# Threshold attention and a gelu feed-forward on one core: the row thresholds of ten score tiles move from adding DMAs to VectorE, under a new set of planner ranks

## The chip, the cores and the metric

The kernel runs on one core of one Trainium2 chip. The time is device microseconds from launch to the last store, taken as the median of several executions. A profiled execution gives the span from the first to the last instruction and what each engine did in it: PE (TensorE; its weight loads are PEld), DVE (VectorE), ACT (ScalarE), POOL (GpSimd) and SP (SyncE). SP and POOL mostly issue DMAs here, each from its own queue.

## The reference

Two stages in fp32. Attention has 8 batches of 8 heads, 576 positions and a head dimension of 64; a score below its row's maximum less tau is dropped before the softmax. Its output, seen as 4608 tokens of 512 values, goes through a feed-forward of width 2048.

```python
scores = scale * np.matmul(q, k.transpose(0, 1, 3, 2))
thresh = np.max(scores, axis=-1, keepdims=True) - tau
scores = np.where(scores >= thresh, scores, -1000000000.0)
scores = scores - np.max(scores, axis=-1, keepdims=True)
attn = np.exp(scores)
attn = attn / (np.sum(attn, axis=-1, keepdims=True) + 1e-09)
...
h = x @ w_in
g = h * (1.0 / (1.0 + np.exp(-1.702 * h)))
return (g @ w_out).astype(np.float32)
```

## The kernel before

**Tiling.** Heads go in pairs n = 0 to 31, four pairs to a batch (`NPAIR`). A pair's transposed scores lie in five tiles t = 0 to 4 in SBUF: four of 128x1152 and a last one of 128x576, half as large ("full" and "half" tiles below).

**One pair's steps.** `load_qk` and `load_v` (SP) bring q, k and v in. For pairs 0 to 3 PE turns q and k (`turn_in`, L566/L569), ACT evacuates q's turn (`turned`, L581) and DVE k's (L579). `scores_run` (PE, L591) makes nine pieces of scores, and `keep` (ACT, L608) copies each out of PSUM. `in_groups` (DVE, L614) takes maxima within each tile, `over_tiles` (L623) over the tiles; `cross_max` (ACT, L633) and `over_halves` (DVE, L640) combine across partitions. The result is each query's threshold. It then reaches all partitions in one of two ways. For most pairs DVE spreads it (`spread_max`, L652). For the pairs in `BY_DMA` (1, 3, 4, 5, 6) DVE turns it to a negated row (`turn_rows`, L647/L648), one DMA stores the row to DRAM (`row_out`, L664) and another reads it back to every partition (`row_in`, L673).

Then comes the step that the change touches: the threshold is taken from every score tile. `sub` (L688) does it on DVE, in place, with the spread threshold as the second operand (an add for the `BY_DMA` pairs, whose row is negated). `add_row` (L679) does it without DVE: POOL issues two DMAs that read the row from DRAM and accumulate it onto the tile in SBUF. The dictionary `ADDED` names the tiles that go that way: tiles 3 and 4 of pairs 1, 3, 4, 5 and 6.

After it `mask` (ACT, L695) sends negative differences far down, `exps` (ACT, L699) takes the exponential, and PE multiplies with v and with ones (`values` and `sums_by_pe`, L710). For pairs 0 to 3 `one_row` (DVE, L741) makes the reciprocal sums and `place_x` (DVE, L814) writes the four blocks of the scaled output where the feed-forward reads its x. PE's feed-forward can begin with a batch's tokens when all four of its pairs are placed.

**Weights.** They come in pieces, packed as pairs of 16-bit halves, and are put together by ACT and DVE: `load_w` (SP), `cv_power` (ACT, L521), `cv_power2` (ACT, L525), `cv_whole` (DVE, L539) and `cv_end` (DVE, L546), in this chain for every piece; `cv_whole` needs the load alone, `cv_end` both others.

**Feed-forward.** Tokens go in 18 blocks of 256. The first two are one group: PE L877/L888 (first product, 16 columns j of the hidden layer, two of which fit PSUM at a time), ACT tanh (L844), DVE `gelu_0` (L894), PE L857 (second product). Later blocks use products of sums and differences of half matrices (L956, L1098, L1397, and L1249 and L1358 for the last four), which need further sums by DVE (L1144, L1263 on ACT, L1266 and others) and prepared weights that POOL moves (`t_minus` L998, `t_plus` L1002, `w_plus` L927, `w_flow` L1075).

**What sets the order.** The schedule is manual. Each step is a task with an engine, an estimated cost, a rank, what it comes after and which buffers it takes and gives. `run_in_order` plays the tasks through once while the program is built: whenever an engine is free in this model, the ready task of lowest rank whose buffers are free is emitted on it. The engines then run what was emitted, each in its own order. A rank is a pair's number plus a bias by the step's name, from one of three dictionaries, `EARLY` for pairs 0 to 3, `SECOND` for pairs 4 to 7 and `LATER` for the rest; `CV` holds the biases of the weight steps, `W_RANK` the ranks of the pieces by groups, `L_RANK` those of the loads of q, k and v of the first eight pairs. So one list of numbers decides where every step stands among the others on its engine:

```python
biases = EARLY if a[0] < NPAIR else SECOND if a[0] < 2 * NPAIR else LATER
rank += CV[f.__name__] if f.__name__ in CV else biases.get(f.__name__, 0.0)
```

and the tile's way is chosen where the tasks of a pair are listed:

```python
if t in mine:
    last_add = task("POOL", 1.3, r, add_row, n, t, after=[last_add] + copies)
    a = transfer("DMW", 2.0 if tail else 4.0, last_add, 1, lag=2.0, ...)
else:
    a = task("DVE", 0.67 if tail else 1.27, r, sub, n, t, after=[y for y, _ in subs], ...)
```

(`mine` is `ADDED.get(n, ())`.) The buffer of the row in DRAM (`row`, one) is given back by the last add of a pair in `ADDED`, and by the transfer of `row_in` for any other; the buffer of the spread threshold is given back by the pair's last `sub`.

Of the kernel before, what the change touches and what calls it, by code (L numbers as in the profile page):

```python
# [32 lines left out]
def kernel(  # L33
# [97 lines left out]
    for x in ("raw0", "raw1", "qkT0", "qkT1", "mb"):  # L131
# [3 lines left out]


    EARLY = {
        "add_row": -35.07,
        "cross_max": 51.78,
        "exps": -47.2,  # L140
        "in_groups": 31.96,
        "keep": 48.24,
        "load_qk": -22.72,
        "load_v": -16.59,
        "mask": 58.66,
        "one_row": 92.6,
        "over_halves": -5.3,
        "over_tiles": 3.55,
        "place_x": -34.81,
        "row_in": -3.02,  # L150
        "row_out": 179.21,
        "scores_run": -83.61,
        "spread_max": -0.55,
        "spread_sums": 83.81,
        "sub": 80.72,
        "sums_by_pe": 70.37,
        "turn_in": 65.21,
        "turn_rows": -10.62,
        "turned": 53.23,
        "values": -17.63,  # L160
    }
    SECOND = {
        "add_row": 6.96,
        "cross_max": 30.38,
        "cross_sums": 55.52,
        "exps": 48.43,
        "in_groups": 180.71,
        "keep": -68.97,
        "load_qk": -48.26,
        "load_v": -36.2,  # L170
        "mask": 36.98,
        "over_halves": -6.02,
        "over_tiles": 2.67,
        "place_x": 82.5,
        "prep": 45.44,
        "row_in": -45.04,
        "row_out": 99.69,
        "scores_run": 89.89,
        "spread_max": 152.36,
        "sub": 70.1,  # L180
        "sums_in": -66.2,
        "sums_out": 19.25,
        "turn_rows": -3.9,
        "turn_sums": 85.81,
        "values": 27.28,
    }
    LATER = {
        "add2": 28.57,
        "add3": -10.19,
        "copy2": 7.59,  # L190
        "copy3": 128.37,
        "cross_max": 33.26,
        "cross_sums": -30.68,
        "exps": 4.78,
        "in_groups": 26.34,
        "keep": -16.52,
        "load_qk": 26.97,
        "load_v": 0.95,
        "mask": -12.52,
        "over_halves": 1.14,  # L200
        "over_tiles": -27.28,
        "place_x": -12.29,
        "prep": 220.24,
        "s_level1": 112.72,
        "s_level2": 77.75,
        "scores_run": -3.6,
        "silu2": 34.02,
        "spread_max": 18.84,
        "sub": -15.73,
        "sums_in": 49.27,  # L210
        "sums_out": 57.21,
        "turn_sums": 100.25,
        "values": -2.28,
    }
    CV = {
        "cv_end": 87.96,
        "cv_power": 26.67,
        "cv_power2": -7.18,
        "cv_whole": 151.72,
        "load_w": 4.18,  # L220
    }

    LAG = {"PE": 0.26, "DVE": 0.18, "ACT": 0.22, "POOL": 0.18, "SP": 0.1}
# [7 lines left out]
    def task(engine, cost, rank, f, *a, after=(), take=(), give=(), lag=None):  # L231
        if lag is None:
            lag = LAG[engine]
        if rank != FIRST and rank < LAST and f not in (first_act, tau_terms, run_up, stay_warm):
            biases = EARLY if a[0] < NPAIR else SECOND if a[0] < 2 * NPAIR else LATER
            rank += CV[f.__name__] if f.__name__ in CV else biases.get(f.__name__, 0.0)
        tasks.append((engine, cost, rank, f, a, [x for x in after if x is not None],
                      take, give, lag))
        return len(tasks) - 1
# [9 lines left out]
    def transfer(by, time, a, kind=0, give=(), lag=1.7):  # L249
        return task(by, time, FIRST, moved, kind, after=[a], give=give, lag=lag)  # L250
# [182 lines left out]
    def own(n, *pools):  # L433
        return tuple(x + "_apart" for x in pools) if n in APART else pools
# [1049 lines left out]

    SUMS_IN_A = 2
    SUMS_BY_PE = (0, 1, 2, 3)
    ADDED = {n: (3, 4) for n in (1, *range(3, 7))}
    BY_DMA = (1, *range(3, SINGLE))
    SUMS_BY_DMA = range(4, NP)
    LEAD = 6  # L1490
# [4 lines left out]
    FFU = 1.727  # L1495
    T_RANK = FIRST

    W_RANK = (-2.54, 76.74, 38.5, 60.86, -18.31, 3.32)
    W_TIME = 1.8
    WARM = 22  # L1500
    ROUND_BY_ACT = range(0)
# [2 lines left out]
    for i in range(len(pieces)):  # L1504
        y = 0 if i < NDC else 2 if i < n_in else 4
        n = NDC if i < NDC else n_in - NDC if i < n_in else n_in
        first = (0, 0, NDC, 0, n_in)[y]
        rank = W_RANK[y] + (W_RANK[y + 1] - W_RANK[y]) * (i - first) / n
        if not wide:
# [732 lines left out]
            next_blk += 1  # L2242

    crossed = {"max": [], "sums": []}
    L_RANK = (-36.67, -8.83, 19.0, 14.55, -8.83, 6.12, -80.2, -13.57, 33.56, 28.6, 36.68, 5.08, 89.16, -23.31, -89.41, -12.49, 50.76, 2.25, -31.08, -35.43, 70.85, 84.46, 108.91, -12.25)

    def load_rank(n, which):
        return L_RANK[3 * n + which] if 3 * n < len(L_RANK) else 0.0

# [15 lines left out]
    for n in range(NP):  # L2265
# [106 lines left out]
        if n in BY_DMA:  # L2372
            a = task("DVE", 0.22, r, turn_rows, n, after=[a])
            a = transfer(rq[2], 0.3 + 0.4 * by_sp, task(rq[0], 0.65 * rq[1], r, row_out, n, after=[a]), lag=1.7 - 0.4 * by_sp + flow)
            spread[n] = task(rq[0], 1.1 * rq[1], r, row_in, n, after=[a], take=own(n, "mb"))
            m = transfer(rq[2], 1.1, spread[n], 0 if by_sp else 1, give=() if n in ADDED else ("row",), lag=rq[3] + flow)
        else:
            m = task("DVE", 0.78, r, spread_max, n, after=[a], take=own(n, "mb"))
        spread.setdefault(n, m)
        ws, subs, last_add = [], [(m, None)], spread[n]  # L2380
        mine = ADDED.get(n, ())
        for t in range(NKT + 1):
# [108 lines left out]
```

## Time and profile before

| | |
|---|---|
| median of 3 runs | 1229.73 us (1229.53 to 1229.79) |
| profiled execution, its own time | 1230.11 us |
| its span | 1228.3 us, TensorE clock 0.999 |
| PE busy | 1212.3 us (99%) |
| PEld busy | 980.9 us (80%) |
| DVE busy | 1059.2 us (86%) |
| ACT busy | 817.5 us (67%) |
| POOL busy | 71.2 us (6%) |
| `sub`, L688 | 150 instructions, 180.2 us |
| `mask`, L695 | 160 instructions, 164.2 us |
| `add_row`, L679 | 20 DMA issues, 18.9 us busy, from 35.9 to 167.8 us; 4.5 to 11.9 us from issue to landing, median 7.8 |
| `row_in`, L673 | 10 DMA issues, 5.3 us busy |

"Busy" is the time in which an engine executes an instruction; "idle before" is the time it stood still ahead of one. DVE's and ACT's records overlap by some 0.08 us when one instruction follows another directly, so the distance of starts says what an instruction costs its engine, not its length. Times within the span are counted from its start. In lists by stretch, the columns after a stretch's length are the busy times of PE, PEld, DVE, ACT and POOL, each with its number of instructions in brackets, then the granted TensorE clock, the mean busy share of the 16 DMA engines and the GB/s they moved; a share above 1 in such a list means that more transfers were under way than there were engines.

### The profile page before, as it was taken

What the parts mean: (1) busy time and instruction counts of PE and PEld (TensorE: products, weight loads), DVE (VectorE), ACT (ScalarE), POOL (GpSimd) and SP (SyncE); (2) the same over time, 40 slices, a digit from 0 to 9 for tenths busy, and PEclk for the clock granted to TensorE, in tenths of its full rate; (3) what the DMA queues carried; (4) which work ended last, traced back from release to release, by engine and by line L of the source; (5) the groups of instructions that cost most, each with busy time, mean ns of one, the idle gap of its engine ahead of it and who ended that gap; (6) DMA issues with size and microseconds to landing.
All of it is one profiled execution on the core that took longest, in us unless ns stands there. A gap on an engine that the chain in (4) does not pass through costs nothing.

```text
span 1228.3 us, 26047 instructions
## 1 busy us (share of the span) xinstructions
PE 1212.3 (99%) x10592; PEld 980.9 (80%) x10592; DVE 1059.2 (86%) x1650; ACT 817.5 (67%) x1203; POOL 71.2 (6%) x115
## 2 busy tenths in 40 slices
PE   9988999999999999999999999999999999999998
PEld 6746764497978888888777777777887797999998
DVE  6998984779898998899699987998789889999797
ACT  7999995786766766685776467756875677340330
POOL 0111213110000000000000010000100000000000
PEclk9999999999999999999999999999999999999999
DMA  7956858793323133224423252224322342344443
GB/s 220 250 109 175 189 122 159 135 210 73 110 49 110 39 92 85 75 74 130 102 66 101 73 129 74 65 64 120 99 49 66 112 113 61 118 131 137 146 126 106
DMA packets 201512, 137.12 MB, mean 112 GB/s; under 512 B 146800, under 2 KB 163184, under 8 KB 201264
## 3 DMA queue, kind: packets, MB, share of 16 engines
q1 hardware_dynamic: 188992, 110.21, 33.4%
q0 software_dynamic: 11712, 24.95, 9.9%
q8 instruction: 83, 1.36, 0.5%
q10 hardware_dynamic: 688, 0.30, 0.1%
q14 instruction: 37, 0.30, 0.1%
HBM read 103.28 MB, written 23.75 MB: 103 GB/s over the span
## 4 chain that ended last, share of the span: by engine, by line
PE 85%; ACT 7%; DVE 5%; DMA 1%; issue 1%; ACTq 0%; DVEq 0%
PE ops L1397 24%; PE pv L710 10%; PE ps L591 10%; PE hps L956 7%; PE hps L1098 7%; PE ps L956 5%; PE ps L1098 5%; PE ops L857 5%; PE ops L1358 3%; PE hps L1249 3%; PE ps L1358 2%; PE ps L1249 2%; DVE arena L1266 2%; PE hps L888 2%; ACT arena L699 2%; ACT arena L695 2%
## 5 line engine op out<-in xcount | busy, mean ns | idle before, releaser
L614 DVE TRANSPOSE_TENSOR_REDUCE part<-arena 128x36 f32<-128x1152 f32 x300 | 364.0, 1240 | 54.2 <-ACT arena L608 43.3
L608 ACT COPY arena<-ps 128x576 f32<-128x576 f32 x288 | 170.4, 644 | 107.8 <-PE ps L591 107.5
L695 ACT ACTIVATE arena<-arena 128x1152 f32<-128x1152 f32 (+1 forms) x160 | 164.2, 1059 | 49.3 <-DVE arena L688 46.0
L699 ACT ACTIVATE arena<-arena,shift,scl 128x1152 f32<-128x1152 f32 (+1 forms) x160 | 193.9, 1245 | 1.2
L688 DVE TENSOR_TENSOR arena<-arena 128x1152 f32<-128x1152 f32 (+1 forms) x150 | 180.2, 1243 | 0.7
L591 PE MATMUL ps<-arena 64*64 64x288 f32 x2304 | 171.1, 408 | 4.0 <-ACT arena L608 3.5
L1397 PE MATMUL ops<-w_out,arena 128*128 128x256 f32 x768 | 174.5, 381 | 0.0
L1397 PEld LDWEIGHTS ops<-w_out,arena 128*128 128x128 f32 x768 | 144.2, 190 | 25.3 <-issue 5.7
L710 PE MATMUL pv<-arena 64*64 64x288 f32 x2176 | 159.7, 405 | 0.0
L591 PEld LDWEIGHTS ps<-arena 64*64 64x64 f32 x2304 | 82.6, 133 | 65.6 <-ACT arena L608 23.8
L710 PEld LDWEIGHTS pv<-arena 64*64 64x64 f32 x2176 | 82.3, 133 | 52.2 <-issue 8.8
L1397 PE MATMUL ops<-arena 128*128 128x256 f32 x528 | 118.1, 379 | 0.0
L1397 PEld LDWEIGHTS ops<-arena 128*128 128x128 f32 x528 | 100.2, 190 | 14.0 <-issue 0.4
L1263 ACT COPY arena<-hps 128x512 f32<-128x512 f32 x44 | 25.7, 583 | 58.5 <-PE hps L1249 44.3
L633 ACT ACTIVATE other<-red,minus_gap 32x18 f32<-32x18 f32 x118 | 36.2, 307 | 34.3 <-DVE red L623 32.7
L857 PE MATMUL ops<-w_out,arena 128*128 128x512 f32 x128 | 55.9, 595 | 0.0
L1075 POOL DMA_DIRECT2D arena<-wrow x36 | 19.4, 540 | 595.9 <-DVE arena L688 298.6
L888 PE MATMUL hps<-xT,w_in 128*128 128x256 f32 x232 | 51.7, 382 | 2.0 <-DVE arena L894 1.9
L888 PEld LDWEIGHTS hps<-xT,w_in 128*128 128x128 f32 x232 | 43.5, 190 | 10.2 <-DVE arena L894 3.6
L857 PEld LDWEIGHTS ops<-w_out,arena 128*128 128x128 f32 x128 | 24.1, 190 | 30.1 <-issue 29.8
L1144 DVE TENSOR_TENSOR arena<-ps,arena 128x512 f32<-128x512 f32 x36 | 23.7, 685 | 26.4 <-PE ps L1098 26.4
L956 PEld LDWEIGHTS hps<-xT,w_in 128*128 128x128 f32 x384 | 44.3, 192 | 0.7 <-issue 0.5
(229 smaller groups left out, 1934.2 us busy)
## 6 DMA issues: line engine op xcount, KB each, us to landing
arena<-in_v_dram SPq DMA_DIRECT2D x128, 144.0 KB
arena<-exu SPq DMA_DIRECT2D x42, 256.0 KB
arena<-ext SPq DMA_DIRECT2D x39, 256.0 KB
arena<-wrow POOLq DMA_DIRECT2D x36, 256.0 KB, 3.0
out_dram<-osb SPq DMA_DIRECT2D x32, 256.0 KB
arena<-in_k_dram SPq DMA_DIRECT2D x112, 72.0 KB
arena<-in_q_dram SPq DMA_DIRECT2D x112, 72.0 KB
arena<-row_s SPq DMA_DIRECT2D x48, 144.0 KB
```

The source lines that it names most:

```text
L591: nc.tensor.matmul(ps[ts(c, KT), h, 0:SH], lhsT=mats[n, 1][ts(h, D), ts(j, KT)], rhs=mats[n, 0][ts(h, D), ts(c, SH)], start=True, stop=True,)
L608: nc.scalar.copy(out=sT[n, t][:, u], in_=pss.pop((n, j))[:, :, 0:SH])
L614: nc.vector.tensor_reduce(out=stats[n, op][:, t * 2 * QB : min(2 * t + 2, NK) * QB], in_=sT[n, t].rearrange("p u h (g d) -> p (u h g) d", ...
L688: engine.tensor_tensor(out=s, in0=s, in1=mbs[n].unsqueeze(1).to_broadcast(list(s.shape)), op=ALU.add if n in BY_DMA else ALU.subtract,)
L695: nc.scalar.activation(out=s, in_=s, func=AF.Prelu, alpha=STEEP)
L699: nc.scalar.activation(out=s, in_=s, func=AF.Exp, scale=scl, bias=shift)
L710: nc.tensor.matmul(o[c][ts(h, D), 0:SH], lhsT=left(j, h)[ts(c, KT)], rhs=sT[n, t][ts(c, KT), u, h, :], start=(j == 0), stop=(j == NK - 1),)
L857: nc.tensor.matmul(acc[i], lhsT=g0[:, j, ts(i, P)], rhs=w_out[:, j, :], start=(j == 0), stop=(j == NFC - 1),)
L888: nc.tensor.matmul(hidden[j][:, ts(i, BLK)], lhsT=w_in[:, c, ts(j, P)], rhs=xTs[i][:, c, :], start=(c == 0), stop=(c == NDC - 1), skip_gro ...
L956: nc.tensor.matmul(o[:, ts(j, HT)], lhsT=left[:, c, ts(4 * y + j, P)], rhs=right[:, c, :], start=(x in (P1, P2, P5) and j + c == 0), stop= ...
L1098: nc.tensor.matmul(o[:, ts(j, BLK)], lhsT=left[:, c, ts(j, P)], rhs=right[:, c, :], start=(x in (P1, P2, P5) and j + c == 0), stop=(j + c ...
L1397: nc.tensor.matmul(banks[blk][k][:, ts(o, HM)], lhsT=left[:, j, :], rhs=right[:, j, :], start=(j == 0), stop=(j == HF - 1),)
```

## The change

`ADDED` becomes empty: the ten `add_row` tasks (20 DMAs on POOL's queue) go, and ten `sub` instructions on DVE come in their place, five on full and five on half tiles. The rows of the five pairs are still stored and read back, since `BY_DMA` stays. All ranks and biases get other values; the two `add_row` entries go with their step. Nothing else is edited, so apart from the twenty DMAs and the ten subtractions the new program has the same instructions in another order.

```diff
@@ -135,89 +135,87 @@
     EARLY = {
-        "add_row": -35.07,
-        "cross_max": 51.78,
-        "exps": -47.2,
-        "in_groups": 31.96,
-        "keep": 48.24,
...
-        "one_row": 92.6,
...
-        "turned": 53.23,
-        "values": -17.63,
+        "cross_max": 38.77,
+        "exps": 109.98,
+        "in_groups": -20.53,
+        "keep": -20.83,
...
+        "one_row": -9.89,
...
+        "turned": -23.63,
+        "values": -53.54,
     }
     SECOND = {
-        "add_row": 6.96,
...
     CV = {
-        "cv_end": 87.96,
-        "cv_power": 26.67,
-        "cv_power2": -7.18,
-        "cv_whole": 151.72,
-        "load_w": 4.18,
+        "cv_end": 39.6,
+        "cv_power": 113.57,
+        "cv_power2": 23.8,
+        "cv_whole": -36.36,
+        "load_w": 73.1,
     }
...
-    ADDED = {n: (3, 4) for n in (1, *range(3, 7))}
+    ADDED = {}
     BY_DMA = (1, *range(3, SINGLE))
...
-    W_RANK = (-2.54, 76.74, 38.5, 60.86, -18.31, 3.32)
+    W_RANK = (3.21, 35.75, 48.86, 53.37, 40.75, -22.25)
...
-    L_RANK = (-36.67, -8.83, 19.0, 14.55, -8.83, 6.12, -80.2, -13.57, 33.56, ...
+    L_RANK = (-29.82, -85.16, -16.59, 33.25, -20.03, -23.65, 107.45, 78.99, 74.94, ...
```

More of the change, by code (lines that the diff above doesn't have):

```diff
@@ L137 @@
     EARLY = {
-        "add_row": -35.07,
-        "cross_max": 51.78,
-        "exps": -47.2,
-        "in_groups": 31.96,
-        "keep": 48.24,
-        "load_qk": -22.72,
-        "load_v": -16.59,
-        "mask": 58.66,
-        "one_row": 92.6,
[L147 to L155, printed above, removed]
@@ L156 @@
-        "sums_by_pe": 70.37,
-        "turn_in": 65.21,
-        "turn_rows": -10.62,
-        "turned": 53.23,
-        "values": -17.63,
+        "cross_max": 38.77,
+        "exps": 109.98,
+        "in_groups": -20.53,
+        "keep": -20.83,
+        "load_qk": -46.1,
+        "load_v": 87.48,
+        "mask": 113.55,
+        "one_row": -9.89,
+        "over_halves": -51.29,
+        "over_tiles": 17.06,
+        "place_x": 31.38,
+        "row_in": 115.99,
+        "row_out": -29.26,
+        "scores_run": 5.81,
@@ L161 @@
+        "spread_max": 108.46,
+        "spread_sums": 114.68,
+        "sub": 61.38,
+        "sums_by_pe": 32.67,
+        "turn_in": 62.83,
+        "turn_rows": -69.51,
+        "turned": -23.63,
+        "values": -53.54,
     }
     SECOND = {
-        "add_row": 6.96,
[L164 to L185, printed above, removed]
+        "cross_max": -6.06,
+        "cross_sums": -86.01,
+        "exps": 133.28,
+        "in_groups": 123.85,
+        "keep": 28.39,
+        "load_qk": -2.14,
@@ L186 @@
+        "load_v": 124.51,
+        "mask": 116.06,
+        "over_halves": 49.78,
+        "over_tiles": 50.9,
+        "place_x": 85.06,
+        "prep": 113.89,
+        "row_in": 37.58,
+        "row_out": -16.51,
+        "scores_run": -39.03,
+        "spread_max": 109.02,
+        "sub": 110.14,
+        "sums_in": 108.79,
+        "sums_out": -52.91,
+        "turn_rows": 81.62,
+        "turn_sums": -27.64,
+        "values": 105.08,
     }
     LATER = {
-        "add2": 28.57,
-        "add3": -10.19,
@@ L190 @@
[L190 to L213, printed above, removed]
+        "add2": -82.78,
+        "add3": -85.4,
+        "copy2": 88.43,
+        "copy3": 23.25,
+        "cross_max": 42.25,
+        "cross_sums": -23.35,
+        "exps": 116.34,
+        "in_groups": 34.9,
+        "keep": -5.4,
+        "load_qk": -49.52,
+        "load_v": 110.88,
+        "mask": 53.19,
+        "over_halves": 101.5,
+        "over_tiles": -13.6,
@@ L214 @@
+        "place_x": 29.07,
+        "prep": 122.2,
+        "s_level1": -23.22,
+        "s_level2": -51.32,
+        "scores_run": 106.62,
+        "silu2": 3.44,
+        "spread_max": 5.07,
+        "sub": 27.41,
+        "sums_in": 118.45,
+        "sums_out": -6.8,
+        "turn_sums": 51.39,
+        "values": -30.24,
     }
     CV = {
-        "cv_end": 87.96,
-        "cv_power": 26.67,
-        "cv_power2": -7.18,
-        "cv_whole": 151.72,
-        "load_w": 4.18,
+        "cv_end": 39.6,
@@ L2244 @@
     crossed = {"max": [], "sums": []}
-    L_RANK = (-36.67, -8.83, 19.0, 14.55, -8.83, 6.12, -80.2, -13.57, 33.56, 28.6, 36.68, 5.08, 89.16, -23.31, -89.41, -12.49, 50.76, 2.25, -31.08, -35.43, 70.85, 84.46, 108.91, -12.25)
+    L_RANK = (-29.82, -85.16, -16.59, 33.25, -20.03, -23.65, 107.45, 78.99, 74.94, 108.02, 46.22, -85.81, 83.93, 9.47, 47.15, -85.66, 110.01, -1.1, 86.09, -18.05, 51.18, 33.29, -0.19, 72.5)
     def load_rank(n, which):
```

## The prediction

> **What bounds the kernel now.** I read the page's 40 slices first, then busy time by stretch, then the chain that ended last, then the timelines around the places where the chain changes engine.
>
> ```profile
> PE   9988999999999999999999999999999999999998
> DVE  6998984779898998899699987998789889999797
> ACT  7999995786766766685776467756875677340330
> ```
>
> ```profile
> 50.00:105.00 55.00, 48.01 (x661) 26.52 (x651) 45.53 (x80) 54.26 (x75) 10.45 (x16) 1.00 0.53 110
> 105.00:168.00 63.00, 61.04 (x382) 49.08 (x379) 58.97 (x91) 60.83 (x90) 13.89 (x22) 1.00 0.81 198
> 168.00:246.00 78.00, 78.00 (x493) 37.66 (x492) 48.85 (x70) 54.47 (x76) 16.63 (x21) 1.00 0.73 135
> 246.00:1050.00 804.00, 804.00 (x6767) 657.78 (x6766) 706.68 (x1007) 554.81 (x803) 22.56 (x38) 1.00 0.35 90
> ```
>
> The columns after the length are PE, PEld, DVE, ACT and POOL busy. Up to 105 us ACT is the wall: 54.26 of 55 us busy, while DVE has 9.5 us free and PE is padded with waiting. From 168 us on PE is the wall: 78.00 of 78, then 804.00 of 804. The stretch between belongs to both, with DVE free for 4.0 us. So the end is the time at which the feed-forward can start on PE, plus a fixed amount of PE work, plus PE's gaps. Whatever ACT or DVE lose before 105 us is paid in full; what they lose after 246 us costs nothing up to the last two blocks. The chain says the same:
>
> ```profile
> 96.89 1.20 PE den L710 x16
> 104.17 8.29 DMA w_out<-in_moe_w_out_dram
> ...
> 116.10 3.72 PE hps L888 x16
> 119.83 17.53 PE hps L888 x80
> ...
> 245.61 3.57 PE hps L956 x32
> ```
>
> The feed-forward (L888) starts at 105.03, when place_x(3), pair 3's last step, ends at 103.55. Its gate:
>
> ```profile
> 98.62 0.87 ACT L699 ACTIVATE arena<-arena,shift,scl 128x576 f32<-128x576 f32 x1
> 99.39 0.75 ACT L521 ACTIVATE w_in<-w_out,rebias 128x512 f32<-128x512 int16 x1
> 100.17 0.72 ACT L525 ACTIVATE w_in<-w_in,rebias 128x512 int32<-128x512 f32 x1
> ```
>
> ```profile
> 100.32 0.85 DVE L741 TRANSPOSE_TENSOR_REDUCE r<-den 128x9 f32<-128x288 f32 x2 [2.10 <-PE den L710]
> 102.60 0.95 DVE L814 TENSOR_TENSOR xT<-pv,arena 128x256 f32<-128x256 f32 x4
> 103.46 1.28 DVE L546 SCALAR_TENSOR_TENSOR w_in<-w_out,w_in 128x512 int32<-128x512 int32 x2
> ```
>
> exps(3,4), the last exponential of pair 3, ends at 99.49; PE adds its sums; one_row(3) on DVE starts at 100.32, 0.83 later, and only after place_x(3) does DVE finish weight piece 8 (L546).
>
> **The change part by part**, on the order in which each kernel's instructions stand on each engine, with durations from these rows. Times are of the profiled span, 1228.3.
>
> *1. Ten DVE subtractions come, ten add transfers of two DMAs each go.* Five whole tiles and five half tiles (pairs 1, 3, 4, 5, 6). L688 instructions on full tiles start 1.27 apart when back to back, and behind a half one (38.17) the next starts at 38.84, 0.67 later: 5 x 1.27 + 5 x 0.67 = 9.7 us of DVE. The four for pairs 1 and 3 (3.9 us) fall before 105 us, into the 9.5 us in which DVE waited. I cost them nothing. If that cover is used up, cross_max(4) on ACT is late: its input was finished by DVE at 94.22 and used at 96.86, 2.6 us of room, so at most 3.9 - 2.6 = +1.3. The other six (5.8 us) fall mostly between 105 and 190 us and are weighed in step 5. POOL loses 20 issues, 18.9 us busy (L679), and nothing else stands on that queue but the rows, so nothing is late for it. The masks of those tiles now wait for DVE and not for a transfer; in the row order DVE is ahead of them.
>
> *2. ACT work ahead of exps(3,4).* The same list, one copy of pair 5 (L608) less: -0.5 us.
>
> *3. ACT's first 35 us.* Before, four weight pieces were converted on ACT at 16.20 and from 29.79 to 34.13 (eight instructions, 5.8 us), filling ACT while pairs 1 and 2 were being made ready. In the new order all four come after mask(0,0), as do two L608 copies and one L581 evacuation: 5.8 + 1.1 + 0.6 = 7.5 us. Without a wait, mask(0,0) would start at 34.49 - 7.5 = 27.0. But ACT now has nothing to do from 15.4, when it has evacuated pair 1's queries, until PE has pair 1's first scores, which PE began at 16.3 before: 1.2 to 1.4 us. And pair 2's first copy now stands behind two turns by PE (q of pair 2, k of pair 3) in place of none; such turns took 1.0 and 1.3 us at 13.77 and 15.20, which with the evacuation between leaves ACT waiting another 1.2 to 1.4 us. I get mask(0,0) at 29.6: +2.6 us. ACT has no free time until 105 us in which to make that up. Bounds: 0, if the new order of loads makes pair 1 ready sooner and every wait closes; +4, if the loads of k for pair 3, which now stand ahead of pair 2's, hold the SP queue for one more such wait.
>
> *4. cv_end(8) now stands ahead of one_row(3) on DVE.* It needs cv_power2(8), which in the new ACT order follows exps(3,4), a copy and cv_power(8): 0.53 + 0.78 + 0.72 = 2.0 us after the exponential, then 0.68 for cv_end itself. one_row(3) starts 2.7 us after exps(3,4) in place of 0.83: +1.9. DVE takes its instructions in order, so nothing behind can pass; what waits is place_x(3) and with it PE. This is the surest term.
>
> *5. 105 to 168 us.* 96 L888 records take 21.14 us where PE runs free; the first 136 took 32.27 where 29.95 were needed, so 2.3 us were lost (waits of 1.04 and 0.86 for gelu_0, L894). The new order puts more DVE work between some gelu_0 steps (up to 5.6 us where PE needs 3.5 per step) and less between others. Bounds: -2.3 if every wait goes, +5.8 if none of the six subtractions finds cover; by DVE's 4.0 us free here, +1.8. I take 0: PE's two score buffers and the earlier conversions on ACT (about 1.5 us less ACT work ahead of the last eight tanh steps) give back what DVE loses.
>
> *Load 16.* Piece 16 took 8.29 us to land at 112.46, and DVE waited 1.45 us for it, on the chain. In the new order its slot is free before place_x(3) and pair 4's four adds, issued from 102.81 to 106.56, are gone; but its cv_whole now stands ahead of gelu_0(0) on DVE. I take it as landed in time. The Trainium skill (Trainium Kernel Development and Optimization, Key Constraints) says that DMAs issued from SP, ACT and POOL run on the same 16 engines and interleave; by that rule the adds' bytes come off this load, and the sum would be up to 1.45 lower. The trace agrees so far that the engines were over-subscribed (share 1.16 at 40 to 50 us) while adds ran.
>
> *6. 168 to 246 us.* PE is gapless. place_x(7) ended at 245.15 and block 2 (L956) began at 245.45, so pair 7 has no room; but a PE that is 4 us late brings that room with it. 0, up to +2 if pair 7 falls further behind.
>
> *7. 246 us to the end.* PE's and DVE's orders are the same but for single swaps until the last four blocks. There PE idles 4.5 us in 178, final stores included, and DVE's sums are reordered: 0, between -1.0 and +1.5.
>
> Sum: -0.5 + 2.6 + 1.9 = +4.0 on 1228.3, so a span of 1232.3. The profiled execution took 1230.11, its span is 1.4 below the median of the runs shown, 1229.73: **1233.7 us**.
>
> **The rivals.** A measurement of this kernel can tell about 0.2% (2.5 us) from no change.
>
> *The early waits close* (step 3 at 0): +1.4, 1231.1, no change by that bound. For it: ACT waited only 0.27 and 0.36 us there before, so preparation was quick. Against: it was quick behind conversions that are now elsewhere.
>
> *DVE becomes the bound between 105 and 190 us.* For it: 58.97 of 63 us busy before and 5.8 to come. Against: 29 us free from 168 to 246. Price 1.8 to 5.8 beyond the forecast, 3.8 in the middle: 1237.5, at most 1239.5. It decides once the gelu_0 steps come more than 3.5 us apart for several steps on end.
>
> *The freed DMA engines pay* (the other side). Without the adds, q, k and weight pieces land sooner: the early waits do not arise, load 16 lands early, the 2.3 us of PE waiting go, and the earlier first gelu_0 steps make up step 4's 1.9. -0.5 - 2.3 = -2.8: 1226.9. For it: the 8.29 us load on the chain. Against: ACT, gapless before 105 us, has the same work, and step 4's wait is for ACT, not for a transfer. It decides if place_x(3) ends no later than 103.5.
>
> **How the numbers follow.** Forecast 0.48, DVE bound 0.19, early waits close 0.24, DMA pays 0.09. So slower 0.67, within 0.2% 0.24, faster 0.09. The likeliest case alone spans 1232.2 to 1236. The range goes down to 1229.0, which leaves out the DMA case and the best of the second, and up to 1239.5, the worst of the DVE case.
>
> **What would show it.** Right: mask(0,0) near 29 to 30 us; exps(3,4) ending near 101.5; one_row(3) 2.7 us behind it with DVE idle before L546; place_x(3) ending near 107.5; block 2's first L956 near 249; PE gapless to 1050. Wrong: L888 starting by 105, or block 2's shift differing from that of L888 by over 2 us, or the tail moving by over 1.5.

## The result, and the profile after

The changed kernel takes 1233.82 us in the median of 19 runs (1230.45 to 1238.03); the kernel before, run 19 times beside it, 1230.14 (1229.43 to 1231.68). The ratio is 1.0026, with a 95% interval of 1.0019 to 1.0033: slower, by 3.7 us from median to median, with a spread some three times as wide. The profiled execution, 1231.06 with a span of 1229.3, is one of the three shortest of the 19, so its trace shows only +1.0 us on the span of before. Two more traced executions of the same kernel (first experiment) took 1232.73 and 1232.99.

Busy time by stretch of the changed kernel (columns as in the prediction; lines from 186 on are two lower than before, so L888 is now L886):

```profile
50.00:105.00 55.00, 47.65 (x644) 25.47 (x636) 46.48 (x80) 54.32 (x75) 4.14 (x8) 1.00 0.40 86
105.00:168.00 63.00, 59.80 (x389) 48.19 (x386) 59.98 (x95) 57.78 (x86) 6.41 (x12) 1.00 0.64 168
168.00:246.00 78.00, 78.00 (x494) 38.02 (x493) 54.32 (x74) 57.96 (x79) 14.94 (x18) 1.00 0.68 126
246.00:1050.00 804.00, 804.00 (x6757) 656.91 (x6755) 704.92 (x1004) 555.58 (x803) 22.52 (x38) 1.00 0.35 90
```

The walls (the engine that is busy almost without a break) stand where they stood: ACT up to 105, PE from 168 to 1050. Only the second stretch differs in kind: PE 59.80 busy for 61.04, ACT 57.78 for 60.83, DVE 59.98 for 58.97. PE and ACT both stand still more, and DVE is fuller by only one us. The table follows a few steps through four traced executions, by their starts and ends in the timelines; it says when the time is lost:

| us from the span's start | before | changed, 1231.06 | 1232.73 | 1232.99 |
|---|---|---|---|---|
| exps(3,4) ends (ACT) | 99.48 | 99.41 | 99.67 | 99.56 |
| place_x(3) ends (DVE) | 103.55 | 105.22 | 105.48 | 105.37 |
| first L888 / L886 (PE) | 105.03 | 106.41 | 106.67 | 106.55 |
| first L857 / L855 (PE) | 167.52 | 169.57 | 171.27 | 171.51 |
| block 2, first L956 / L954 | 245.45 | 247.56 | 249.26 | 249.51 |
| last four blocks, first L1249 / L1247 | 1042.46 | 1044.57 | 1046.25 | 1046.52 |
| span | 1228.3 | 1229.3 | 1231.0 | 1231.2 |

So +1.4 to +1.6 us at the feed-forward's start, +0.7 to +2.5 between it and L855, nothing from there to 1042, and -1.1 in the tail: +1.0, +2.7 and +2.9 on the span. The chain of the changed kernel's first trace (start, length, what) points at the DMAs of the stage between 139 and 170:

```profile
138.84 0.61 DVE w_out L544
...
142.55 11.07 DMA arena<-in_moe_w_out_dram
153.64 4.77 DMA arena<-in_q_dram
158.40 0.41 DVE arena L537
...
162.54 7.19 PE hps L886 x32
```

A conversion frees a buffer at 139.4, SP can then ask for the next weight pieces, and one takes 11.07 us to land. In the kernel before the chain's only long DMA between 90 and 255 us was the 8.29 us at 104.17. The chain goes through that weight piece, but DVE did not stand still for it in this execution: its L537 follows directly on a subtraction, and it is this one that had waited, for pair 5's threshold row, a DMA of POOL's queue in the same stretch:

```profile
157.11 1.36 DVE L686 TENSOR_TENSOR arena<-arena 128x1152 f32<-128x1152 f32 x1 [2.19 <-DMA arena<-row]
```

SP's waits (what for, us in total, times, longest) say why so many transfers meet there, before and after in the 70 us from 100 on:

```profile
SPq L511 <- DVE w_out L539: 16.9, 2, 15.6
```

```profile
SPq L509 <- DVE w_out L544: 22.8, 1, 22.8
```

Before, SP's longest stand lasted to 144.27, and then it sent one piece, and the next at 148.31. Now it stands from 116.5 to 139.47 and then sends six pieces within 3.6 us. The 16 DMA engines lie idle and are then flooded (last two columns: share, GB/s):

```profile
118.00:124.00 6.00, 5.78 (x27) 4.77 (x26) 6.00 (x9) 5.93 (x9) 0.00 (x0) 1.00 0.29 34
124.00:130.00 6.00, 6.00 (x29) 5.29 (x28) 6.00 (x8) 6.00 (x8) 0.00 (x0) 1.00 0.00 0
130.00:136.00 6.00, 6.00 (x31) 4.98 (x34) 5.96 (x8) 5.94 (x10) 0.00 (x0) 1.00 0.00 0
...
148.00:154.00 6.00, 6.00 (x29) 5.29 (x28) 6.00 (x15) 4.65 (x8) 1.05 (x2) 1.00 1.05 329
```

The kernel before has 0.89, 1.08, 0.46 and 1.02 in these four stretches. In the new order cv_power(16) and cv_end(16) stand late (136.7 to 140.2 in the execution of 1232.73, against 113.6 to 117.9 before); load 22 needs their buffer and stands at the head of SP's queue; when it is let go, the six weight pieces go out in one burst, with v (from 144.24) and q (from 148.79) behind them.

What follows was measured with orders written out: where an experiment below moves a step, the planner runs unchanged, its order is recorded, the named tasks are moved in it, and the steps are emitted from the list.

```diff
-                tasks[i][3](*tasks[i][4])
+                order.append(i)
...
+        for i in order:
+            tasks[i][3](*tasks[i][4])
```

`behind(a, b)` takes task a out of the list and puts it directly behind b. In each expectation, "theory" and "rival" are the outcomes that were weighed against each other. Every experiment was timed beside the kernel before, whose medians there were 1230.34 to 1230.45; variants are compared by their medians, and where their runs overlap a difference of 2 us is not settled.

### The profile page after: what moved, and what is told of

It reads as the page before. It is cut to its first block, busy times and chain, and to the rows that moved or that the text cites. A ratio compares the mean times of both kernels' runs of the same rounds, so it can differ in the third digit from the quotient of the medians.

```text
span 1229.3 us, 25991 instructions
## 1 busy us (share of the span) xinstructions
PE 1211.5 (99%) x10592; PEld 979.8 (80%) x10592; DVE 1068.5 (87%) x1660; ACT 818.7 (67%) x1203; POOL 51.9 (4%) x95
## 4 chain that ended last, share of the span: by engine, by line
PE 87%; ACT 7%; DVE 4%; DMA 2%; SPq 0%; issue 0%; DVEq 0%; ACTq 0%
PE ops L1395 24%; PE pv L708 10%; PE ps L589 9%; PE hps L954 7%; PE hps L1096 7%; PE ps L954 5%; PE ps L1096 5%; PE ops L855 5%; PE ops L1356 4%; PE hps L1247 4%; PE ps L1356 3%; PE ps L1247 3%; ACT arena L697 2%; ACT arena L693 2%; ACT arena L606 1%; DVE part L612 1%
## 5 line engine op out<-in xcount | busy, mean ns | idle before, releaser
L686 DVE TENSOR_TENSOR arena<-arena 128x1152 f32<-128x1152 f32 (+1 forms) x158 | 189.8, 1239 | 3.7 <-DMA arena<-row 3.1
L855 PE MATMUL ops<-w_out,arena 128*128 128x512 f32 x128 | 55.9, 595 | 0.0
L886 PE MATMUL hps<-xT,w_in 128*128 128x256 f32 x232 | 51.4, 381 | 3.1 <-DVE arena L892 3.1
L886 PEld LDWEIGHTS hps<-xT,w_in 128*128 128x128 f32 x232 | 43.6, 190 | 11.0 <-DVE arena L892 4.4
L855 PEld LDWEIGHTS ops<-w_out,arena 128*128 128x128 f32 x128 | 24.0, 190 | 30.2 <-issue 29.5
L954 PEld LDWEIGHTS hps<-xT,w_in 128*128 128x128 f32 x384 | 44.3, 192 | 0.7 <-issue 0.5
L954 PE MATMUL hps<-xT,w_in 128*128 128x128 f32 x384 | 44.8, 275 | 0.0
```

Source lines behind the costliest of these rows:

```text
L686: engine.tensor_tensor(out=s, in0=s, in1=mbs[n].unsqueeze(1).to_broadcast(list(s.shape)), op=ALU.add if n in BY_DMA else ALU.subtract,)
L855: nc.tensor.matmul(acc[i], lhsT=g0[:, j, ts(i, P)], rhs=w_out[:, j, :], start=(j == 0), stop=(j == NFC - 1),)
L886: nc.tensor.matmul(hidden[j][:, ts(i, BLK)], lhsT=w_in[:, c, ts(j, P)], rhs=xTs[i][:, c, :], start=(c == 0), stop=(c == NDC - 1), skip_gro ...
L954: nc.tensor.matmul(o[:, ts(j, HT)], lhsT=left[:, c, ts(4 * y + j, P)], rhs=right[:, c, :], start=(x in (P1, P2, P5) and j + c == 0), stop= ...
```

## The experiments

**1. The changed kernel again, two traced executions (after_a, after_b).** No edit.

> The changed kernel as it is, one more profiled execution. Its timed runs go from 1230.45 to 1238.03, while the profiled one took 1231.06 (span 1229.3, PE's second block group starting at 247.56). Theory: what varies is the landing of DMAs between 139 and 162 us (weight pieces, pair 5's threshold row), because SP's queue stood for 22.8 us and then sent its loads in a bunch; an execution of 1233 or more then shows the feed-forward start (L886) at 106.4 within 0.3, DVE waiting for pair 5's row (L686 on pair 5, 2.19 us in the first trace) 2 us or more longer, and block 2 (L954) at 250 or later, with the tail unchanged. Rival: the early loads of q and k vary, and L886 itself starts at 108 or later. Second rival: the four last blocks vary, and block 2 stays at 247.6.

> The same kernel once more, for the same question: where an execution that takes longer loses its time. Theory, DMAs between 139 and 162 us: block 2 shifts with the time of the execution, L886's start does not. Rival, the early loads: both shift alike. Second rival, the tail: neither shifts.

They took 1232.73 and 1232.99, so just short of the 1233 that the expectation set as its condition. The theory held in place: L886 within 0.3 of the first trace, the tail the same, and block 2 later, though at 249.26 and 249.51 and not at 250. DVE's timeline of the second execution, with its idle time and what ended it:

```profile
107.44 0.43 DVE L537 TENSOR_SCALAR w_out<-w_out 128x512 int32<-128x512 uint32 x1 [0.87 <-DMA w_out<-in_moe_w_out_dram]
150.06 0.43 DVE L537 TENSOR_SCALAR arena<-arena 128x512 int32<-128x512 uint32 x1 [2.26 <-DMA arena<-in_moe_w_out_dram]
159.06 1.36 DVE L686 TENSOR_TENSOR arena<-arena 128x1152 f32<-128x1152 f32 x1 [0.82 <-DMA arena<-row]
```

DVE waits 3.95 us for DMAs here, 3.71 in the execution of 1232.73 (0.39, 2.18, 1.14), 2.19 in the first (pair 5's row alone): so 1.8 us more (1232.99) and 1.5 more (1232.73), and block 2 is 1.95 and 1.70 later. In the detail the expectation missed: it named a longer wait for the row, and it was mostly weight pieces 16 and 23 at cv_whole.

**2. The subtractions alone, replanned (subs).**

```diff
 # kernel before
-    ADDED = {n: (3, 4) for n in (1, *range(3, 7))}
+    ADDED = {}
```

> The kernel before with ADDED empty and its own ranks: the ten subtractions alone, in the order that the old ranks give. Theory (the subtractions hide, the order costs): the new order puts cv_end(9) ahead of one_row(3), behind cross_max(4), cv_power(9) and cv_power2(9), so place_x(3) ends 2 us later than before, and block 2 begins about 2 us later: 1231 to 1233. Rival (DVE pays for the ten subtractions after 105 us): gelu_0 steps are late, PE waits 4 us or more between 105 and 168, 1234 to 1239. Second rival (freed DMA engines pay): 1228 or less.

1256.65 us, ratio 1.0214 (1.0200 to 1.0228), beyond every expectation. With the old ranks the planner puts the products of pair 8 with v, and pair 9's scores between them, ahead of block 2's first products, where the kernel before has them behind; place_x(4) comes at 187.7 in place of 154.7 and place_x(7) at 269.3 in place of 245.2. PE stands still (PE timeline of this kernel), and its clock between 256 and 272 us is 0.50:

```profile
258.42 1.77 PE L710 MATMUL pv<-arena 64*64 64x288 f32 x4 [8.99 <-ACT arena L699]
...
269.56 1.24 PE L591 MATMUL ps<-arena 64*64 64x288 f32 x8 [5.68 <-ACT arena L608]
```

Experiment 3 makes the same ten subtractions in the old order and loses 3 us, so most of the 26 us belong to the replanned order: with this planner an edit can't be priced by replanning with the old ranks. All runs below but ranks, later and tail7 hold an order fixed.

**3. The subtractions alone, order fixed (subs_fixed).** In the order of before, each pair's two adds become subtractions placed behind its third one (pair 4's tile 3 one place earlier).

```diff
 # kernel before
+        for n in ADDED:
+            for t in (3, 4):
+                i = names["add_row", n, t]
+                order.remove(i)
+                order.insert(order.index(names["sub", n, t - 2 if n == 4 else 2]) + 1, i)
...
     def add_row(n, t):
-        s = sT[n, t].rearrange("p u h s -> p u (h s)")
...
+        sub(n, t)
```

> The kernel before, its order step for step, with the ten adding transfers replaced by ten subtractions on DVE, each behind the pair's last subtraction (pair 4's third tile one place earlier); no other step moves. The 26 us of the kernel with replanned order would then be the planner's. Theory (hidden up to 105 us, DVE nearly full between 105 and 168): L888 starts as before within 0.5, block 2 (L956) 0 to 3 us later, time 1230 to 1233. Rival (DVE bound): 1233 to 1237. Second rival (freed DMA engines pay): 1229 or less.

1233.33 us, ratio 1.0025 (1.0015 to 1.0035), between theory and rival. Against before, in its trace: ACT's cross_max(2) waits 1.00 us for DVE at 55.04, beyond the 0.4 that this execution began with, and place_x(3) follows; gelu_0(2) is 0.16 earlier than before, because the 1.45 us of DVE waiting for load 16 are gone; then subtractions of pairs 4 and 5 put gelu_0(10) 3.6 late, and L857 starts 2.86 late. All three mechanisms are there at once: 1.0 before 105 us, -1.5 for the freed DMA engines, about +3 after it, 2.5 us in this trace.

**4. The adds put back, replanned (ranks) and with the order fixed (adds_fixed).** The first is the changed kernel with the old `ADDED`; the second keeps its order and only exchanges the ten steps.

```diff
 # changed kernel, adds_fixed
+        for n in ADD:
+            for t in (3, 4):
+                order.remove(names["sub", n, t])
...
         mbs[n] = mb
+        for t in (3, 4):
+            add_row(n, t)
...
+    ADD = (1, *range(3, 7))
```

> The changed kernel with ADDED as it was before: the new ranks with the adding transfers back. cv_end(8) stands ahead of one_row(3) here too. Theory (the order costs, the subtractions do not): L886 starts 1.4 us later than before, as in the changed kernel, and the time is 1231 to 1235. Rival (the subtractions cost): the time is back within 0.8 us of the kernel before.

> The changed kernel's order, step for step, with tiles 3 and 4 of pairs 1, 3, 4, 5, 6 again done by adding transfers (issued right behind row_in) and their ten subtractions left out of DVE's list. Theory (the subtractions are hidden in the new order): L886 starts as in the changed kernel (106.4) within 0.5, and the time is 1232 to 1236, not lower by more than 1. Rival (the ten subtractions cost what they last after 105 us, 5.8): 1228 to 1230. Second rival (the adds' bytes delay weights and rows further): 1236 or more.

1237.53 us, 1.0050 (1.0036 to 1.0063), and 1237.03 us, 1.0048 (1.0035 to 1.0061). ranks lies beyond both of its expectations: replanned, it is another order again (L886 starts at 105.68), and says little of the subtractions. For adds_fixed the second rival was right: L886 starts as in the changed kernel (106.54), but the adds' bytes meet the weights, and DVE waits for DMAs seven times between 82 and 171 us, among them:

```profile
109.72 0.43 DVE L551 TENSOR_SCALAR arena<-arena 128x512 int32<-128x512 uint32 x1 [1.40 <-DMA arena<-in_moe_w_out_dram]
116.55 0.43 DVE L551 TENSOR_SCALAR arena<-arena 128x512 int32<-128x512 uint32 x1 [1.45 <-DMA arena<-in_moe_w_out_dram]
...
161.73 1.36 DVE L702 TENSOR_TENSOR arena<-arena 128x1152 f32<-128x1152 f32 x1 [3.09 <-DMA arena<-row]
```

With orders fixed the four medians are:

| | adds | subtractions |
|---|---|---|
| old order | 1230.3 | 1233.3 |
| new order | 1237.0 | 1233.8 |

The two parts of the change are not a sum. In the old order the exchange of adds for subtractions costs 3 us, and no run of either kernel reaches into the other's, timed side by side; in the new order it brings 3 from median to median, though the five runs with adds (1233.63 to 1238.09) overlap those of the changed kernel. The new order costs 6.7 us with adds and 0.5 with subtractions.

**5. cv_end(8) behind place_x(3) (no_cv8), and then cv_whole(16) and (17) out of the way too (n2).**

```diff
 # changed kernel, order list
+        behind(("cv_end", 8), ("place_x", 3))
+        behind(("load_w", 16), ("cv_end", 8))
+        behind(("load_w", 17), ("load_w", 16))
 # n2 only
+        behind(("cv_whole", 16), ("in_groups", 5, 2))
+        behind(("cv_whole", 17), ("cv_whole", 16))
```

> The changed kernel's order with one step moved: cv_end(8) directly behind place_x(3) (and load 16, which needs its buffer, behind it; SP's own order stays). Theory: DVE no longer waits 2.1 us for cv_power2(8), place_x(3) ends 1.5 to 1.9 earlier (103.5) and L886 starts near 105.0; but piece 16 is asked for 1.5 us later and cv_whole(16) stands ahead of gelu_0(0), so part comes back as a wait for that load as in the kernel before (1.45 us there): 0.5 to 1.5 us less than the changed kernel, 1232.3 to 1233.3. Rival: everything behind follows the start of the feed-forward, 1.4 to 1.9 less. Second rival: the load decides, no gain or a loss.

> The kernel in which cv_end(8) stands behind place_x(3), with one more edit: cv_whole(16) and cv_whole(17) stand behind gelu_0(1) and two in_groups, in place of ahead of gelu_0(0). The loads go out as late as in that kernel, but DVE no longer stands at piece 16 while gelu_0(0) is ready. Theory (in that kernel DVE's 4.2 us at cv_whole(16) were the whole loss, and the early place_x(3) is worth what was forecast): gelu_0(0) near 108, L886 start 105.0 to 105.9, 1231.5 to 1234. Rival (the later request for piece 16 and those behind it costs by itself, in later waits): 1236 or more, most of the loss stays.

no_cv8: 1239.06 us, 1.0071 (1.0058 to 1.0084), all five runs at 1237.76 or more. DVE's timeline of it:

```profile
101.11 0.85 DVE L753 TRANSPOSE_TENSOR_REDUCE r<-den 128x9 f32<-128x288 f32 x2 [1.98 <-PE den L722]
...
110.30 0.43 DVE L551 TENSOR_SCALAR w_out<-w_out 128x512 int32<-128x512 uint32 x1 [4.16 <-DMA w_out<-in_moe_w_out_dram]
```

place_x(3) ends only 0.9 earlier (104.34), since one_row(3) still waits 1.98 for PE. In both orders PE makes a score piece ahead of pair 3's last sums; before, it started at 98.88, while the last exponential was still running, and here it starts at 99.85, because the copy by ACT that frees its buffer now stands behind that exponential (99.18 to 99.80). And piece 16, asked for at 104.97 in place of 102.11, holds DVE for 4.16 us: the second rival was right, and the expectation's "part comes back" was far too small. The step that looked like a pure loss bought an earlier load. n2 takes DVE's wait away, gelu_0(0) is back at 108.09, and the median is 1235.35, 1.0041 (1.0029 to 1.0053): 3.7 of the 5.2 us come back, not all; that it stays 1.5 above the changed kernel is not settled, since their runs overlap. In its trace (1236.42) pair 5's row is 3.01 us late at 159.65, and PE then shows this (busy time by stretch, clock in the third column from the end; then PE's timeline):

```profile
160.00:166.00 6.00, 2.31 (x9) 1.71 (x8) 5.93 (x10) 4.43 (x6) 1.02 (x2) 0.85 0.38 127
166.00:172.00 6.00, 6.00 (x18) 4.80 (x17) 5.38 (x8) 4.05 (x6) 1.07 (x2) 0.58 0.86 232
```

```profile
165.07 7.28 PE L902 MATMUL hps<-xT,w_in 128*128 128x256 f32 x19 [3.69 <-DVE arena L908]
```

PE waits 3.69 us and then runs twelve matmuls 0.427 us apart in place of 0.216: the wait is paid almost twice (12 x 0.21 = 2.5 us more).

**6. Loads earlier (early16).** Pieces 16 and 20 change places in cv_power, cv_power2 and cv_end.

```diff
 # changed kernel, order list
+        for f in ("cv_power", "cv_power2", "cv_end"):
+            swap(f, 16, 20)
```

> The changed kernel's order with pieces 16 and 20 exchanged in the three conversion steps (cv_power, cv_power2, cv_end), so that the buffer that SP's queue waits for (load 22) comes free 3 us earlier, near 136.5 in place of 139.5. Same work, same places. Theory (late DMAs cost 2 to 4 us of DVE waiting between 139 and 159, and make the time vary): the wait of cv_whole(23), 2.2 us, and part of that for pair 5's row, 0.8 to 2.2 us, go: 1.5 to 3 us less than the changed kernel, 1231 to 1232.3, and less spread than its 1230.45 to 1238.03. Rival (the DMA engines' share decides, not the time of the request): same time within 0.6.

1235.80 us, 1.0044 (1.0030 to 1.0058); its runs, 1233.35 to 1237.84, overlap those of the changed kernel. DVE's waits for piece 23 and for pair 5's row are gone from the trace, as expected, but the burst now meets pair 4's sums, a small DMA of POOL's queue, at place_x(4):

```profile
153.85 0.95 DVE L829 TENSOR_TENSOR xT<-pv,arena 128x192 f32<-128x192 f32 x4 [3.36 <-DMA arena<-row_s]
```

So an earlier request does remove these two waits, but the burst that is moved collides with the next transfer. That the waits for DMAs cost the changed kernel its time is not shown by this run, which is no faster.

**7. Waiters moved out of the way (late23).**

```diff
 # changed kernel, order list
+        behind(("tanh", 9), ("cv_power2", 22))
+        behind(("gelu_0", 9), ("tanh", 9))
+        behind(("sub", 5, 0), ("gelu_0", 12))
+        behind(("sub", 5, 1), ("sub", 5, 0))
+        behind(("mask", 5, 0), ("sub", 5, 1))
+        behind(("exps", 5, 0), ("mask", 5, 0))
+        behind(("sub", 5, 2), ("gelu_0", 13))
+        behind(("sub", 5, 3), ("sub", 5, 2))
```

> The changed kernel's order with waiters moved out of the way, no load moved: tanh(9) ahead of cv_power(23) on ACT, gelu_0(9) ahead of cv_whole(23) on DVE, and pair 5's first four subtractions behind gelu_0(12) and gelu_0(13) (its first mask and exponential with them). Theory (instructions that stand behind a late DMA, though they do not need it, lose 2 to 4 us in the median execution between 139 and 162 us): mm2 (L855) starts 3 to 5 us earlier than in the executions of 1232.7 and 1233.0, near 167; 1229 to 1231.5, with less spread. Rival (PE or the weights themselves are needed at those places): within 1 us of the changed kernel's 1233.8, or DVE's and ACT's waits only move on to the next instruction.

1237.07 us, 1.0052 (1.0041 to 1.0063): the theory fell, and L855's counterpart starts at 175.49, not near 167. The trace (1239.71, the longest of six) shows the second half of the rival: gelu_0(12) is freed, but on ACT the mask now stands ahead of tanh(13):

```profile
164.63 1.17 ACT L712 ACTIVATE arena<-arena 128x1152 f32<-128x1152 f32 x1 [2.75 <-DVE arena L705]
...
168.14 0.57 ACT L861 ACTIVATE xT<-hps 128x512 f32<-128x512 f32 x1
```

The wait moved to the next instruction, and pairs 5 to 7, which have no room before block 2, got later still (place_x(7) ends at 253.26). Not all of this execution's loss is the moved steps': DVE also waited 0.89 and 1.59 us for pieces 16 and 17, at 107.09 and 110.45, and PE then 3.35 us.

**8. The tail (later, tail7).** The kernel before with all new `LATER` ranks, then with only the seven that belong to steps of the last four blocks.

```diff
 # kernel before, tail7
-        "add2": 28.57,
-        "add3": -10.19,
-        "copy2": 7.59,
-        "copy3": 128.37,
+        "add2": -82.78,
+        "add3": -85.4,
+        "copy2": 88.43,
+        "copy3": 23.25,
...
-        "s_level1": 112.72,
-        "s_level2": 77.75,
+        "s_level1": -23.22,
+        "s_level2": -51.32,
...
-        "silu2": 34.02,
+        "silu2": 3.44,
```

> The kernel before with the new kernel's LATER ranks alone. The order is that of before up to about 155 us (first difference at cv_whole(27)) and that of the changed kernel from about 260 us on. Theory (the last four blocks gain 1.1 us by the new order, PE's stalls of 1.2 us at 1108 to 1112 go): 0.8 to 1.3 less than the kernel before, and PE without a wait at 1108 to 1112. Rival (the steps between 155 and 260 us that move too cost as much): within 0.4 of it.

> The kernel before with seven of the new LATER ranks, those of the steps that only the last four blocks have (add2, add3, copy2, copy3, s_level1, s_level2, silu2). The order is that of before up to block 14 and the changed kernel's from there on. Theory (the tail's new order is worth 1.1 us, and it was the 1.0 us between 246 and 272 us that hid it in the run with all LATER ranks): 0.9 to 1.3 us less than the kernel before (about 1229.2), PE without the stalls at 1108 and 1111. Rival (the tail's gain needs the new order of the steps ahead of it): within 0.4 of the kernel before.

later: 1230.27 us, 0.9999 (0.9990 to 1.0007). Its trace is 1.24 late at 1042 and 0.10 late at the end, so the tail gains 1.14; about as much (1.04) is lost between 246 and 272 us, most of it (0.77) at 264, where PE waits for a copy by ACT (L970). tail7: 1229.49 us (1228.69 to 1230.08, 11 runs) against 1230.35 (1229.45 to 1231.33): 0.9994 (0.9985 to 1.0003). The 0.86 us agree with the theory's 0.9 to 1.3, but the interval just reaches no change. Its trace gains 1.14 us behind 1042, and these two waits of PE in the kernel before have no counterpart in it:

```profile
1108.82 1.16 PE L1358 MATMUL ops<-arena,arena 128*128 128x128 f32 x8 [0.37 <-ACT osb L1364]
1111.43 1.16 PE L1358 MATMUL ops<-arena 128*128 128x128 f32 x8 [0.56 <-DVE arena L1314]
```

It has the lowest median of all versions that were run, though not clear of the kernel before.

## Why the prediction was right, and where it was not

The median, 1233.82, is near the forecast's 1233.7, and the sign is right, but the sum came out by terms that cancel: that it came so near is luck. By the prediction's own signs the mechanism was not right. The last exponential of pair 3 was to end near 101.5 and place_x(3) near 107.5; they end at 99.41 to 99.67 and at 105.22 to 105.48. And one sign of being wrong came up in two of the three traced executions: block 2's shift differs from that of the feed-forward's start by 2.17 us (3.81 against 1.64) and 2.54 (4.06 against 1.52), in the first by 0.73.

*Steps 2 and 3, -0.5 and +2.6: step 3 is wrong.* exps(3,4) ends at 99.41 against 99.48; the two came to -0.1, where +2.1 was forecast. ACT's new waits in the first 35 us are there (0.91, 0.32 and 0.85, together 2.1 us; before had 0.22, 0.27 and 0.36, together 0.85), but ACT's first copy starts at 8.94 for 9.40, because k of pair 0 is now loaded first, and mask(0,0) stood at 28.03, not 29.6. Waits that grew by 1.2, less 0.46 for the earlier copy and 0.5 for step 2, make +0.3; the rest, 0.3 us, is not traced. The rival "the early waits close" had this size (step 3 at 0), but not this way: the waits did not close.

*Step 4, +1.9: right in time, wrong in its price.* place_x(3) ends 1.67 later than before, and DVE waits for just the step named:

```profile
98.55 0.87 ACT L697 ACTIVATE arena<-arena,shift,scl 128x576 f32<-128x576 f32 x1
...
100.64 0.72 ACT L523 ACTIVATE w_in<-w_in,rebias 128x512 int32<-128x512 f32 x1
```

```profile
101.39 0.69 DVE L544 SCALAR_TENSOR_TENSOR w_in<-w_out,w_in 128x512 int32<-128x512 int32 x1 [2.12 <-ACT w_in L523]
102.00 0.84 DVE L739 TRANSPOSE_TENSOR_REDUCE r<-den 128x9 f32<-128x288 f32 x2
```

But no_cv8 shows that cv_end(8)'s own share is 0.9: without it one_row(3) waits for PE's score piece, held up by the copy that step 2 booked as 0.5 us gained on ACT. And without it the kernel is 5.2 us slower. "This is the surest term" priced a wait and not the load that the wait pays for.

*Step 1, hidden: so in the new order, not by itself.* In the changed kernel's first trace ACT has no wait between 24 and 105 us, so the four subtractions ahead of 105 cost it nothing. In the old order subs_fixed puts 1.0 us on the path before 105 and about 3 after it, less 1.5 for load 16. The 1.0 is within the bound named in step 1, +1.3, but it was cross_max(2) and not cross_max(4) that waited.

*Step 5, 0 between -2.3 and +5.8: the term that was mis-sized.* From the first L888 to the first L857 before took 62.49 us, the changed kernel 63.16, 64.60 and 64.96: +0.7, +2.1 and +2.5, and the last two go with DVE's longer waits for DMAs (3.71 and 3.95 us in place of 2.19). The step weighed DVE's fullness and PE's pace; by these traces it is SP's queue, which stood for 22.8 us and whose burst then held DVE at instructions ahead of gelu_0. No run took these waits away and won the time, so that they are the whole of it is argued, not shown. *Load 16, in time:* yes in two executions, 0.87 us late in the third. That the adds' bytes come off this load, the rule that the prediction took from the Trainium skill (Trainium Kernel Development and Optimization, Key Constraints), agrees with subs_fixed, where the 1.45 us are gone without another step moved.

*Step 6, 0:* right (77.99 us from L855 to L954, 77.93 before). *Step 7, 0 between -1.0 and +1.5:* -1.1, shown by tail7 to be the order of the last four blocks.

In the first traced execution the sum is +1.4 + 0.7 + 0 - 1.1 = +1.0, in the other two +2.7 and +2.9. The last 0.8 to 1.0 us of the medians' 3.7 are in no trace. Of the rivals, "DVE becomes the bound" named the right stretch with the wrong cause, and "the freed DMA engines pay" is true in part: by its median adds_fixed is 3.2 us slower than the changed kernel. No execution of the changed kernel above 1233 has a trace here, so that those lose their time as n2 and no_cv8 do is inferred from their clock (below).

## What to carry to other kernels

On an engine that takes its instructions in order, an early wait can be the price of an early load: before counting it as a loss, look which buffer the waiting step frees and which DMA queue stands for it. A queue's long standing in one stretch can be paid in the next, when its transfers go out together; read SP's waits and the DMA share by stretch along with the engines' busy times. And where a list scheduler decides the order, price one edit with the order held fixed: replanned, ten subtractions looked like 26 us, with the old order fixed they were 3.

## What the hardware showed that was not expected

A wait of PE of 2 us or more was often, but not always, followed by a clock at half speed. After 5.18 us (no_cv8) ten matmuls start 0.427 us apart instead of 0.216, after 3.69 (n2) twelve, after 3.35 (late23) five, after 2.02 (early16) seven, after 2.00 (no_cv8, at 168.58) eight, after 2.27 (adds_fixed) six; but after 2.07 us (the changed kernel's first trace) and 2.29 (ranks) none. The stretch of early16 behind its 2.02 us:

```profile
156.00:162.00 6.00, 5.62 (x18) 4.67 (x19) 5.96 (x12) 3.33 (x6) 0.00 (x0) 0.72 0.11 37
```

The Trainium skill (TensorE: Matmul & The Clock Gate, "HAM oscillation") warns of idle gaps above about 3.4 us and, in its Part 1, says that the window in which activity is counted runs freely; that gaps of the same length end either way agrees with the free window, while the gaps near 2 us that were punished do not agree with 3.4 as a limit. The changed kernel sits at that edge, with PE waits of 1.5 to 2.1 us at 162 to 164 us in its three traces. Of its 19 runs, ten have a mean clock of 1.000 and take 1230.45 to 1233.96, median 1231.8; nine have 0.996 to 0.999 and take 1233.82 to 1238.03, median 1235.4. Of the 54 runs of before beside the experiments 51 show 1.000 and three 0.999. That fits its wide spread, as a mechanism inferred from these clocks. A mean of 0.999 alone does not prove such a wait: the traced execution of before has it, with a clock of 1.00 from 1200 to 1227 us and of 0.50 in the last 1.3 us, when PE's work is done.
